# Attention steps of a fused kernel: block sums sent on at once, x transposed ahead of P in eight steps, routing tables a step later

## The chip, the cores and the metric

The program runs on one core of a Trainium2 chip. The metric is device time in microseconds, the median of several executions. The engines are called here as in the profile: PE is TensorE (PEld its weight loads), DVE is VectorE, ACT is ScalarE, POOL is GpSimd, SP is SyncE, which issues most transfers.

## The reference

Windowed attention with block summaries, and then a mixture of experts on its output. Cut to what matters:

```
# attention: q, k, v are (4, 8, 768, 64); block 32, window 16
k_sum = max over each block of 32 keys;  v_sum = mean over each block of 32 values
scores = [ scale*q@k.T where |i-j| < 16 else -1e9 ,  scale*q@k_sum.T + log(32) ]
a = softmax(scores);  x = a @ concat(v, v_sum)          # then (3072, 512)
# experts: w1 (8, 512, 1024), w2 (8, 1024, 512)
noisy = x@w_gate + log1p(exp(x@w_noise)) * noise
top2, weights = the two largest of 8 per row, softmax over the two
out[row] += weight * (relu(x[row] @ w1[e]) @ w2[e])     # for both experts of the row
```

## The kernel before, in words

**Steps.** The 3072 rows are 24 tiles of 128 (6 tiles for each of 4 batches). The attention part is a loop over steps `t`. In a step TensorE does, in this order: masks and scores of tile `t+2` (`mask_sums`, `scores`, L316 and L326), `av(t)` (P times V, 32 matmuls, L364), extras, the transposition of P of tile `t+1` (`p_trans`, two halves, L347), and the transposition of the finished x of tile `t-1` (`x_pe`, L418), each of which ScalarE copies out of PSUM (L350, and `x_copy`, L424). VectorE does the maxima for the softmax of tile `t+2` (`smax`, L335, L336), the division of tile `t` (`norm`, L395 to L399: r, ri, x) and extras. ScalarE does the exponentials (`sexp`, L341). GpSimd copies local keys and splits x into two halves (`norm_hi`, `norm_lo`, L405, L410). SyncE issues, in program order, the loads of q (`load_q`), of the value rows of tile `t+2` (`v_load`, L296, L297), and the write of finished x to memory (`x_out(t-2)`, L413). PSUM tiles for `p_trans`, `x_pe` and some extras come from a ring of three (`pt_space`).

**Extras** are hung on steps by a table, `at(step + fraction, function, ...)`. `run(step + fraction)` calls them at set places of the step; the fraction chooses the place, .4 and .1 are VectorE's (`.4` woven with `norm`, `.1` behind it). They are:
- For each of batches 1 to 3: key maxima (`k_piece`, `kmax`, L232, steps `KP`), loads of all value rows (`load_vn`, in the tile `hth`, L145, steps `VL`), the block sums of values by 48 small matmuls (`v_sums_pe`, L266, steps `VS`), their copy by ScalarE (`v_sums_out`, L278), and one transfer that repeats them for the other window slots (`v_rest`, `vw<-vw` or `htl<-htl`, L288). `av` of the batch's first tile (6, 12, 18) needs them.
- The weights of the first expert: `w_load(0, i)` loads, `w_part` splits into a high half on ScalarE (L736) and a low one on VectorE (L734).
- The routing of each four tiles: logits by TensorE (`gate_gt`, L438, in steps 5, 9, 13, 17, 21, and `gate_gl`, L449, a step later), the choice of two experts (`gate_b`, `gate_m`, L477 to L500), positions (`gate_c` to `gate_e`, L514 to L559, then `gate_q` on GpSimd), and a table product that sorts rows by expert: `lh` (L591), `oc` (L623), `rh` (L630) on VectorE, `gate_t` (L642) on TensorE, `gate_u` (L646, adds to `acc`) on VectorE.
- When three tables are in, `decode` (L653 to L659) gives the row numbers of the first expert's first three groups of 128; `x_gather` fetches those rows (an indirect transfer by GpSimd, `xg<-xd`, L94), `x_trans` transposes them by a transfer (`xte<-xg`, L861). The first expert's matmuls (L883) start behind the loop and read `xte`.

Behind that, eight experts follow one another, TensorE's matmuls back to back. None of it is touched.

Of the kernel before, what the change touches and what calls it, by code (L numbers as in the profile page):

```python
# [21 lines left out]
P = 128  # L22
# [29 lines left out]
GROUP0 = 3  # L52
# [10 lines left out]
def attn_moe(ctx, tc, qt, kt, vt, wgn, noise, w1, w2, out):  # L63
# [517 lines left out]
    GR = {}  # L581

    def gate_lh(b, h=0):
        if h and b == LASTB:
            lh = HT[0][:, :, H0:H0 + P]
        else:
            lh = work.tile([P, 2 * GN, P], F16, name="lh", bufs=1)
        GR[b, h] = [lh]
        shape = [P, 2 * GN, P // 2, 2]
        rf = G[b][2][:, GN * h:GN * h + GN].rearrange("p t k two -> p (t k) two")  # L590
        nc.vector.tensor_tensor(lh.rearrange("p a (c two) -> p a c two", two=2),  # L591
                                pairs_of(iotar)[:, None].to_broadcast(shape),
                                rf[:, :, None, :].to_broadcast(shape), op=OP.is_equal)
# [19 lines left out]
    def gate_o(b, h=0):  # L613
        val, qf, rf = G[b]
        oc = work.tile([P, GN, 2, NS], F16, name="oc", bufs=1)
        if h and b == LASTB:
            rh = HT[1][:, :, H0:H0 + 3 * NS]
        else:
            rh = work.tile([P, 2 * GN, 3 * NS], F16, name="rh", bufs=1)
        ic = iotac.rearrange("p e c -> p (e c)")  # L620
        qk = qf[:, GN * h:GN * h + GN].rearrange("p t k two -> p (t k) two")
        shape = [P, 2 * GN, NS // 2, 2]
        nc.vector.tensor_tensor(oc.rearrange("p t k (c two) -> p (t k) c two", two=2),  # L623
                                pairs_of(ic)[:, None].to_broadcast(shape),
                                qk[:, :, None, :].to_broadcast(shape), op=OP.is_equal)
        GR[b, h] += [rh, oc]

    def gate_f(b, h=0):
        _, rh, oc = GR[b, h]
        nc.vector.tensor_tensor(  # L630
            rh, oc.rearrange("p t k c -> p (t k) c")[:, :, None, :].to_broadcast([P, 2 * GN, 3, NS]),
            G[b][0][:, GN * h:GN * h + GN].rearrange("p t k v two -> p (t k v) two")[:, :, None, :].to_broadcast(
                [P, 6 * GN, NS // 2, 2]), op=OP.mult)

    def gate_t(b, o, hs=(0,), i=1):
        tb = o[:, i, GO:GO + 3 * NS]
        n = 2 * GN * len(hs)
        for h in hs:
            lh, rh, _ = GR[b, h]
            for j in range(2 * GN):  # L640
                n -= 1
                nc.tensor.matmul(tb, lh[:, j], rh[:, j], start=(h == hs[0] and j == 0), stop=(n == 0),  # L642
                                 skip_group_check=True)
# [448 lines left out]
    def at(t, f, *a):  # L1092
        todo.setdefault(round(t, 3), []).append((f, a))
# [23 lines left out]
    at(0.2, v_sums_out, 0)  # L1117

    w_alloc(0)
    for i, (l, h, z) in enumerate(((6, 8, 9), (7, 9, 10), (15, 19, 20), (16, 20, 21))):  # L1120
        at(l, w_load, 0, i)
        for k in range(2):
            at(h + 0.9, w_part, i, k, 0)
            at(z + 0.1, w_part, i, k, 1)
    VS = [4, 9, 15]
    KP = ((1, 1, 2, 2), (5, 6, 7, 8), (10, 12, 13, 14))
    KL = ((-1, 0), (3, 5), (9, 10))
    VL = [(1, 2), (6, 7), (12, 13)]
    for b in range(B - 1):
        for h in range(HP):  # L1130
            at(KP[b][h] + 0.1, k_piece, b + 1, h)
            if h % 2 == 0:
                at(KL[b][h // 2], load_k, b + 1, h, 2)
        for i in range(2):
            at(VL[b][i], load_vn, b + 1, i)
        at(VS[b] + 0.3, v_sums_pe, b + 1)
        at(VS[b] + 0.35, v_sums_out, b + 1)
        at(VS[b] + 1.02, v_rest, b + 1)
    for i in range(4, 8):
        at((17.9, 18.9, 21.9, 22.9)[i - 4], w_load, 0, i)  # L1140
    for i in range(3):
        at(4.9 + 2 * i, fill, i)
    at(20.8, last_init)
# [7 lines left out]
    def choose(b, t, m, c):  # L1151
        at(4 * b + 6 + 0.6, gate_a, b)
        if t == m:
            at(t + 0.4, lambda b: both(gate_b(b), gate_m(b)), b)
        else:
            at(t + 0.4, gate_b, b)
            at(m + 0.4, gate_m, b)
        at(m + 0.9, gate_p, b)
        at(c + 0.3, lambda b, t: gate_c(b, PO[t]), b, c)
        at(c + 0.4, lambda b, t: both(gate_d(b, PO[t]), gate_e(b)), b, c)  # L1160
        at(c + (1.7 if b < 1 else 0.7), gate_q, b)
# [2 lines left out]
        for g in gens:  # L1164
            yield from g

    choose(0, 7, 8, 9)
    choose(1, 11, 12, 13)
    choose(2, 15, 15, 16)
    choose(3, 20, 21, 22)  # L1170

    def make_table(b, v, lh, oc, rh):
        at(v + 0.8, gate_v, b, False)
        at(lh + 0.1, gate_lh, b)
        at(oc + 0.1, gate_o, b)
        at(rh + 0.1, gate_f, b)
        at(rh + 1.3, lambda b, t: gate_t(b, PO[t], (0,)), b, rh + 1)
        at(rh + 1.4, lambda b, t: gate_u(b, PO[t]), b, rh + 1)

    make_table(0, 10, 11, 11, 12)  # L1180
    make_table(1, 13, 14, 14, 15)
    make_table(2, 16, 17, 17, 18)
    at(19.1, decode, TB0, 0, 3)
    at(22.6, gate_a, 4)
    at(22.8, gate_v, 3, False)

    def run(t):
        for f, a in todo.pop(round(t, 3), []):
            f(*a)
# [13 lines left out]
        weave(small, more)  # L1203

    for c in range(3):
        at((20.25, 20.25, 20.7)[c], x_gather, 0, c, P * BATCH[GROUP0][0])
        at((21.02, 21.02, 21.8)[c], x_trans, 0, c)

    HI_ACT = ()

    for t in range(-2, NT - 1):
        u = t + 3
        if 4 <= t + QA < NT:
            load_q(t + QA)
        if 1 <= t < NT - 2:
            v_load(t + 2)
        if t >= 2:
            x_out(t - 2)
        run(t + 0.02)
        if t + 2 < NT:  # L1220
            mask_sums(t + 2)
            scores(t + 2)
        if 1 < u < NT and t < 1:
            q_piece(u)
        if u < NT and t >= 1:
            kx_sum(u)
            kx_local(u)
        run(t + 0.25)
        if t >= 1:
            norm_hi(t - 1, t - 1 not in HI_ACT)  # L1230
            norm_lo(t - 1)
        if t + 2 < NT:
            smax(t + 2)
        if t == 0:
            p_trans(1, 0)
            p_trans(1, 1)
        run(t + 0.2)
        if t >= 0:
            av_space(t)
            av(t)  # L1240
        run(t + 0.3)
        if t + 2 < NT:
            sexp(t + 2, 0)
        run(t + 0.35)
        if t == -1 or t > 0:
            p_trans(t + 1, 0)
            p_trans(t + 1, 1)
        if t >= 1:
            x_pe(t - 1)
        run(t + 0.09)  # L1250
        if t + 2 < NT:
            sexp(t + 2, 1)
        vector_work(t)
        if t >= 1:
            x_copy(t - 1)
        run(t + 0.6)
        run(t + 0.7)
        run(t)
        run(t + 0.8)
        run(t + 0.9)  # L1260
        run(t + 0.95)
# [311 lines left out]
```

## Time and profile before

| what | us |
|---|---|
| median of 3 runs (lowest, highest) | 650.5 (649.82, 651.01) |
| profiled execution, its own time | 652.03 |
| its span, first to last instruction | 650.2 |
| TensorE busy | 627.2 (96%) |
| VectorE busy | 480.0 (74%) |
| ScalarE busy | 306.3 (47%) |
| GpSimd busy | 351.3 (54%) |

The mean granted clock of TensorE was 0.997 of full speed. The loop with the 24 steps takes about the first 132 us. The busy shares are means over parts with different limits: what the loop waits for has to be read from the loop's own rows.

### The profile page before, as it was taken

How to read it: one execution, taken by the hardware profiler on the slowest of the kernel's cores; microseconds unless marked ns; L12 is line 12 of the kernel's file. 1: busy time of each engine (PE TensorE's matmuls, PEld its weight loads, DVE VectorE, ACT ScalarE, POOL GpSimd, SP SyncE). 2: the span in 40 equal slices, each digit the busy share in tenths (PEclk: the TensorE clock that was granted, in tenths of full speed). 3: DMA queues.
4: the chain of work that ended last, by engine and by line, in shares of the span. 5: the costliest groups of instructions: out<-in, count | busy, mean ns of one | idle time of the engine just before them, and what ended most of it. 6: DMA issues, size and time to landing. Idle time of an engine off the chain costs nothing.

```text
span 650.2 us, 14115 instructions
## 1 busy us (share of the span) xinstructions
PE 627.2 (96%) x5407; PEld 369.2 (57%) x5407; DVE 480.0 (74%) x897; ACT 306.3 (47%) x647; POOL 351.3 (54%) x531
## 2 busy tenths in 40 slices
PE   8888888989999999999999999999999999999996
PEld 7777777755555554554455446544554555455543
DVE  7756998987787789587957795788678677856511
ACT  4687777952532553265236523542464155315400
POOL 5575677743836558563765365555556451632042
PEclk9999999999999999999999999999999999999999
DMA  9999998899998676456835573667267723431021
GB/s 316 350 303 363 314 306 276 208 335 307 270 187 173 199 193 178 170 177 159 202 127 189 154 230 125 188 157 242 90 184 164 235 69 113 146 128 49 2 97 55
DMA packets 104568, 125.63 MB, mean 193 GB/s; under 512 B 58393, under 2 KB 59681, under 8 KB 104492
## 3 DMA queue, kind: packets, MB, share of 16 engines
q1 hardware_dynamic: 92348, 88.37, 46.6%
q0 software_dynamic: 12144, 36.28, 17.5%
q8 instruction: 44, 0.72, 0.5%
q14 instruction: 32, 0.26, 0.1%
HBM read 87.38 MB, written 26.21 MB: 175 GB/s over the span
## 4 chain that ended last, share of the span: by engine, by line
PE 74%; issue 8%; DVE 8%; DMA 4%; POOL 3%; ACT 1%; POOLq 1%; SPq 0%; DVEq 0%; ACTq 0%
PE pt L1038 33%; PE h L919 23%; PE h L883 4%; PE a L919 4%; PE pt L1035 3%; PE o L364 2%; DMA hth<-in_vt_dram 2%; PE s L326 1%; DVE s L335 1%; POOL prev L94 1%; PE pt L347 1%; ACT p L341 1%; DVE kmax L232 1%; PE h L1038 1%; DMA xg<-xd,tb 1%
## 5 line engine op out<-in xcount | busy, mean ns | idle before, releaser
L94 POOL DMA_INDIRECT out_dram<-y,tb x48 | 65.8, 1371 | 151.4 <-DVE y L1061 140.7
L1038 PEld LDWEIGHTS <-hth 128*128 128x128 f16 x768 | 74.9, 98 | 89.1
L94 POOL DMA_INDIRECT xg<-xd,tb x53 | 71.2, 1344 | 33.5 <-DMA out_dram<-prev 17.5
L1038 PE MATMUL pt<-w2l,hth 128*128 128x512 f16 x376 | 88.8, 379 | 0.0
L1038 PE MATMUL pt<-w2h,hth 128*128 128x512 f16 x376 | 88.8, 379 | 0.0
L1038 PE MATMUL pt<-w2h,htl 128*128 128x512 f16 x376 | 88.8, 379 | 0.0
L919 PE MATMUL h<-tx,sh 128*128 128x402 f16 x336 | 77.8, 333 | 0.0
L1061 DVE SCALAR_TENSOR_TENSOR y<-pt,tb,prev 128x512 f32<-128x512 f32 x42 | 31.5, 749 | 52.4 <-PE pt L1038 52.4
L741 DVE SCALAR_TENSOR_TENSOR w2l<-stg,w2h 128x1024 f16<-128x1024 f32 x32 | 48.7, 1531 | 28.4 <-ACT w2h L724 28.4
L341 ACT ACTIVATE p<-s,nm 128x120 f32<-128x120 f32 x188 | 53.2, 389 | 25.9 <-DVE nm L336 20.9
L1038 PEld LDWEIGHTS <-htl 128*128 128x128 f16 x384 | 37.5, 98 | 45.3
L919 PEld LDWEIGHTS <-w1h 128*128 128x128 f16 x448 | 43.1, 97 | 33.0 <-issue 1.4
L94 POOL DMA_INDIRECT prev<-out_dram,tb x42 | 51.9, 1236 | 13.6 <-issue 13.6
L788 POOL TENSOR_TENSOR t<-xte 128x804 f32<-128x804 f16 x24 | 38.9, 1645 | 36.7 <-DVE t L744 31.5
L919 PE MATMUL h<-xte,w1h 128*128 128x402 f16 x224 | 56.3, 333 | 0.0
L941 ACT ACTIVATE p<-h 128x402 f32<-128x402 f32 x28 | 14.2, 507 | 74.0 <-PE h L919 72.4
L816 ACT ACTIVATE tx<-t 128x804 f16<-128x804 f32 x28 | 23.7, 869 | 50.4 <-DVE t L744 50.4
L919 PEld LDWEIGHTS <-sh 128*128 128x128 f16 x336 | 32.6, 97 | 24.8
L919 PE MATMUL h<-tx,sl 128*128 128x402 f16 x168 | 42.2, 332 | 0.0
L335 DVE TENSOR_REDUCE s<-s 128x4 f32<-128x480 f32 x47 | 30.9, 658 | 10.1 <-PE s L326 9.8
L927 DVE SCALAR_TENSOR_TENSOR htl<-h,hth 128x402 f16<-128x402 f32 x56 | 31.9, 570 | 8.4 <-ACT hth L924 8.3
L769 ACT ACTIVATE sh<-ws 128x1536 f16<-128x1536 f32 x14 | 20.8, 1482 | 36.2 <-DVE ws L744 28.1
(240 smaller groups left out, 1238.4 us busy)
## 6 DMA issues: line engine op xcount, KB each, us to landing
stg<-in_w_dram SPq DMA_DIRECT2D x62, 512.0 KB, 4.2
q<-in_qt_dram SPq DMA_DIRECT2D x24, 256.0 KB, 6.3
hth<-in_vt_dram SPq DMA_DIRECT2D x8, 768.0 KB, 8.5
xd<-xr SPq DMA_DIRECT2D x24, 256.0 KB, 5.1
out_dram<-prev SPq DMA_DIRECT2D x8, 768.0 KB, 5.3
kb<-in_kt_dram SPq DMA_DIRECT2D x6, 768.0 KB, 6.1
htl<-in_vt_dram SPq DMA_DIRECT2D x12, 260.0 KB, 6.8
vw<-in_vt_dram SPq DMA_DIRECT2D x12, 260.0 KB, 7.8
```

The source lines that it names most:

```text
L94: return nc.gpsimd.indirect_dma_start(**kw)
L335: nc.vector.tensor_reduce(m, SC[t, a], axis=AX.X, op=OP.max)
L341: nc.scalar.activation(PE_[t, a][:, hp, :], SC[t, a][:, hp, :], AF.Exp, bias=NM[t][:, a, hp:hp + 1], scale=SCALE)
L741: nc.vector.scalar_tensor_tensor(lo, SG[e, i], sc, hi, op0=OP.mult, op1=OP.subtract)
L769: nc.scalar.activation(h, x, AF.Copy, scale=W1S)
L788: nc.gpsimd.tensor_tensor(tt(e, 0 if low else j), xb(e, *i, low), xb(e, *o, low), op=OP.subtract)
L816: nc.scalar.activation(TX[e][:, 0, j - 1], t_of(e, j), AF.Copy)
L883: nc.tensor.matmul(ph[:, :n], w[wn][:, c, f * P:(f + 1) * P], x[:, xo + c, c0:c1], start=(k == 0), stop=(k == 11), skip_group_check=hook i ...
L919: nc.tensor.matmul(o, lhs[a][:, c], rhs[b][:, c], start=start and n == 0, stop=stop and n == 5, skip_group_check=True)
L927: nc.vector.scalar_tensor_tensor(HT[1][:, f, c0:c1], c, 0.0, HT[0][:, f, c0:c1], op0=OP.max, op1=OP.subtract)
L1038: nc.tensor.matmul(py, hx[:, f, c * P:c * P + P], w[:, f, :], start=first, stop=final, skip_group_check=True)
L1061: nc.vector.scalar_tensor_tensor(y, py[:, :d], gw, pv[:, :d], op0=OP.mult, op1=OP.add)
```

## The change

Nothing is added or taken out; work is placed elsewhere.
- `v_rest` goes from the step behind the sums (fraction 1.02) to their own step (0.36), directly behind ScalarE's copy. The sums of the third batch (`VS[1]`) go from step 9 to step 10; its load stays.
- In eight steps (4, 5, 9, 10, 13, 15, 17, 21) `x_pe` and `x_copy` stand ahead of `p_trans`.
- VectorE's extras: the first table's parts go from steps 11, 11, 12 to 13, 14, 15, the second's from 14, 14, 15 to 16, 17, 17, the third's from 17, 17, 18 to 18, 18, 19; choices and positions from 7, 8, 9 to 9, 9, 10 (batch 0), 11, 12, 13 to 11, 13, 15, and 15, 15, 16 to 15, 16, 17. One key maximum goes from step 6 to 5. Splits and loads of the first expert's weights are later and further apart.
- `decode` goes from step 19 to 20, the gathers from 20 (the third late in it) to 21, their transposes from 21 to 22, where a new `run(t + 0.01)` puts them ahead of `x_out`.

```
     w_alloc(0)
-    for i, (l, h, z) in enumerate(((6, 8, 9), (7, 9, 10), (15, 19, 20), (16, 20, 21))):
+    for i, l in enumerate((7.8, 10.8, 14, 16)):
         at(l, w_load, 0, i)
-        for k in range(2):
-            at(h + 0.9, w_part, i, k, 0)
-            at(z + 0.1, w_part, i, k, 1)
-    VS = [4, 9, 15]
-    KP = ((1, 1, 2, 2), (5, 6, 7, 8), (10, 12, 13, 14))
+    for i, k, h, z in ((0, 0, 9, 10), (0, 1, 9, 10), (1, 0, 13, 18), (1, 1, 13, 19), (2, 0, 17, 21), (2, 1, 17, 21),
+                       (3, 0, 20, 22), (3, 1, 20, 22)):
+        at(h + 0.9, w_part, i, k, 0)
+        at(z + 0.1, w_part, i, k, 1)
+    VS = [4, 10, 15]
+    KP = ((1, 1, 2, 2), (5, 5, 7, 8), (10, 12, 13, 14))
...
         at(VS[b] + 0.35, v_sums_out, b + 1)
-        at(VS[b] + 1.02, v_rest, b + 1)
+        at(VS[b] + 0.36, v_rest, b + 1)
     for i in range(4, 8):
-        at((17.9, 18.9, 21.9, 22.9)[i - 4], w_load, 0, i)
+        at((17.9, 19.9, 22.8, 22.9)[i - 4], w_load, 0, i)
...
-    choose(0, 7, 8, 9)
-    choose(1, 11, 12, 13)
-    choose(2, 15, 15, 16)
+    choose(0, 9, 9, 10)
+    choose(1, 11, 13, 15)
+    choose(2, 15, 16, 17)
     choose(3, 20, 21, 22)
...
-    make_table(0, 10, 11, 11, 12)
-    make_table(1, 13, 14, 14, 15)
-    make_table(2, 16, 17, 17, 18)
-    at(19.1, decode, TB0, 0, 3)
+    make_table(0, 11, 13, 14, 15)
+    make_table(1, 15, 16, 17, 17)
+    make_table(2, 17, 18, 18, 19)
+    at(20.1, decode, TB0, 0, 3)
...
-        at((20.25, 20.25, 20.7)[c], x_gather, 0, c, P * BATCH[GROUP0][0])
-        at((21.02, 21.02, 21.8)[c], x_trans, 0, c)
+        at(21.25, x_gather, 0, c, P * BATCH[GROUP0][0])
+        at(22.01, x_trans, 0, c)
...
+    EXTRA = sorted(set(VS + [4 * g + 5 for g in range(5)]))
...
+        run(t + 0.01)
         if t >= 2:
             x_out(t - 2)
...
+        run(t + 0.36)
+        if t in EXTRA:
+            x_pe(t - 1)
+            x_copy(t - 1)
         if t == -1 or t > 0:
             p_trans(t + 1, 0)
             p_trans(t + 1, 1)
-        if t >= 1:
+        if t >= 1 and t not in EXTRA:
             x_pe(t - 1)
...
-        if t >= 1:
+        if t >= 1 and t not in EXTRA:
             x_copy(t - 1)
```

The rest of the diff lets `GR` hold a table's parts by name, so that `lh` and `oc` can be made in any order.

What this does to the instructions of an engine shows in the engine's own order. On SyncE, at the block sums of the second batch (steps 4 and 5; L288 is `v_rest`, L118 a load of q, L296 and L297 a `v_load`, L413 an `x_out`):

```order
 L413 DMA xd<-xr 128x1024
+L288 DMA vw<-vw 24x5x520
 L118 DMA q_101<-in_qt_dram 128x512
 L296 DMA vw<-in_vt_dram 64x2x520
 L297 DMA vw<-in_vt_dram 32x2x520
 L413 DMA xd<-xr 128x1024
-L288 DMA vw<-vw 24x5x520
```

`v_rest` moved ahead of one query block's load, one `v_load` and one `x_out`.

On VectorE, around `decode` (L646 is `gate_u`, L395 to L399 the division, L477 to L485 the choice of batch 3, L653 to L659 the decode). Before, in step 19:

```order
L646 TENSOR_TENSOR acc<-acc,o 128x168
L395 TENSOR_SCALAR r<-o 128x8
L397 RECIPROCAL ri<-r 128x8
L399 TENSOR_TENSOR x<-o,ri 128x512
L653 SCALAR_TENSOR_TENSOR oc<-acc 128x3
```

After, in step 20:

```order
L646 TENSOR_TENSOR acc<-acc,o 128x168
L395 TENSOR_SCALAR r<-o 128x8
L477 TENSOR_TENSOR nz<-sp,noi 128x32
L397 RECIPROCAL ri<-r 128x8
L479 SCALAR_TENSOR_TENSOR nl<-lg,nz 128x32
L399 TENSOR_TENSOR x<-o,ri 128x512
L482 MAX mx<-nl 128x8 x4
L485 MAX_INDEX ix<-mx,nl 128x8 x4
L653 SCALAR_TENSOR_TENSOR oc<-acc 128x3
```

The decode stands a step later, and the choice of batch 3, which was in step 20 already, now stands ahead of it.

On GpSimd, the three gathers of the first expert (L94), among the splits of x (L405, L410) and three small fills (L829 to L831). Before:

```order
L94 DMA xg_157<-xd,tb_173 128x1024
L93 MEMSET spacer 1x1
L94 DMA xg_158<-xd,tb_173 128x1024
L405 CAST xr<-x 128x512
L410 TENSOR_TENSOR xr<-x,xr 128x512
L93 MEMSET spacer 1x1
L94 DMA xg_159<-xd,tb_173 128x1024
```

After:

```order
L94 DMA xg_157<-xd,tb_173 128x1024
L93 MEMSET spacer 1x1
L94 DMA xg_158<-xd,tb_173 128x1024
L93 MEMSET spacer 1x1
L94 DMA xg_159<-xd,tb_173 128x1024
```

The third gather no longer stands behind a split of x; all three stand a step later.

## Rows read from the trace of the kernel before

**Rows 1.** Busy time by stretch: stretch, length, PE, PEld, DVE, ACT, POOL, clock, DMA share, GB/s.
```profile
150.00:165.00 15.00, 15.00 (x88) 7.83 (x86) 9.54 (x22) 2.61 (x5) 8.06 (x11) 1.00 0.90 286
```
**Rows 2.** TensorE's timeline in the loop: start, length, instructions, idle before and releaser.
```profile
46.22 1.15 PE L364 MATMUL o<-vw,pts 120*64 120x65 f32 x30 [1.61 <-DMA vw<-vw]
...
61.77 0.96 PE L266 MATMUL pt<-hth 128*24 128x130 f32 x25 [1.70 <-DMA hth<-in_vt_dram]
...
71.07 0.66 PE L418 MATMUL pt<-ident,x 128*128 128x128 f32 x4 [0.90 <-ACT lg L454]
...
81.00 0.35 PE L316 MATMUL s<-mask,identb 64*64 64x384 bf16 x2 [1.09 <-ACT p L341]
...
82.38 1.15 PE L364 MATMUL o<-htl,pts 120*64 120x65 f32 x32 [0.20 <-issue]
...
114.23 1.15 PE L364 MATMUL o<-vw,pts 120*64 120x65 f32 x32
...
118.42 1.15 PE L364 MATMUL o<-vw,pts 120*64 120x65 f32 x32
...
132.60 0.81 PE L883 MATMUL s<-xte,w1h 128*128 128x384 f16 x4 [0.17 <-DMA xte<-xg]
```
**Rows 3.** The chain that ended last: start, length, what.
```profile
41.01 5.17 DMA vw<-vw
...
51.81 9.92 DMA hth<-in_vt_dram
...
123.24 5.29 DMA xg<-xd,tb
128.54 4.02 DMA xte<-xg
```
**Rows 4.** VectorE's timeline in the loop.
```profile
71.46 1.28 DVE L734 SCALAR_TENSOR_TENSOR w1l<-stg,w1h 128x512 f16<-128x512 f32 x2
...
83.16 1.75 DVE L630 TENSOR_TENSOR rh<-oc,val 128x1344 f16<-128x1344 f16 x1
...
99.49 0.85 DVE L630 TENSOR_TENSOR rh<-oc,val 128x1344 f16<-128x1344 f16 x1
...
116.35 0.16 DVE L395 TENSOR_SCALAR r<-o 128x8 f32<-128x8 f32 x1
...
117.46 0.15 DVE L653 SCALAR_TENSOR_TENSOR oc<-acc 128x3 f32<-128x3 f32 x1
...
120.17 0.15 DVE L395 TENSOR_SCALAR r<-o 128x8 f32<-128x8 f32 x1
...
122.10 2.11 DVE L734 SCALAR_TENSOR_TENSOR w1l<-stg,w1h 128x512 f16<-128x512 f32 x2
```
**Rows 5.** SyncE's timeline, the issue of the repeated sums.
```profile
41.01 0.97 SPq L288 DMA_DIRECT2D vw<-vw  x1
```
**Rows 6.** ScalarE's timeline, its copy of the second batch's sums.
```profile
36.76 1.11 ACT L278 ACTIVATE vw<-pt 24x130 f32<-24x130 f32 x4 [0.38 <-PE pt L266]
```
**Rows 7.** Busy time by stretch (columns as in rows 1), in the loop.
```profile
44.30:46.20 1.90, 0.31 (x6) 0.17 (x2) 1.56 (x4) 1.46 (x6) 1.90 (x4) 1.00 0.88 278
59.95:61.75 1.80, 0.12 (x5) 0.00 (x0) 0.00 (x0) 1.22 (x6) 1.72 (x4) 1.00 1.06 353
62.80:66.00 3.20, 3.20 (x42) 2.77 (x35) 1.14 (x6) 1.49 (x6) 0.00 (x0) 0.50 1.01 294
82.38:118.42 36.04, 32.73 (x709) 27.98 (x709) 32.14 (x98) 28.52 (x94) 25.70 (x50) 1.00 0.85 281
```
**Rows 8.** The same table from the start on, for the last two columns.
```profile
0.00:62.00 62.00, 53.58 (x1113) 45.17 (x1117) 44.31 (x132) 42.30 (x132) 40.25 (x88) 1.00 1.00 334
0.00:75.00 75.00, 65.68 (x1340) 55.77 (x1341) 54.20 (x156) 51.88 (x162) 45.46 (x101) 0.98 1.00 332
75.00:80.00 5.00, 4.86 (x86) 3.86 (x85) 4.93 (x24) 3.29 (x11) 4.84 (x9) 1.00 1.01 293
```
**Rows 9.** GpSimd's timeline, the second gather.
```profile
120.18 1.00 POOL L94 DMA_INDIRECT xg<-xd,tb  x1 [0.20 <-issue]
```

More of the change, by code (lines that the diff above doesn't have):

```diff
@@ L587, in gate_lh @@
             lh = work.tile([P, 2 * GN, P], F16, name="lh", bufs=1)
-        GR[b, h] = [lh]
+        GR.setdefault((b, h), {})[0] = lh
         shape = [P, 2 * GN, P // 2, 2]
@@ L625, in gate_o @@
                                 qk[:, :, None, :].to_broadcast(shape), op=OP.is_equal)
-        GR[b, h] += [rh, oc]
+        GR.setdefault((b, h), {}).update({1: rh, 2: oc})
     def gate_f(b, h=0):
-        _, rh, oc = GR[b, h]
+        rh, oc = GR[b, h][1], GR[b, h][2]
         nc.vector.tensor_tensor(
@@ L638, in gate_t @@
         for h in hs:
-            lh, rh, _ = GR[b, h]
+            lh, rh = GR[b, h][0], GR[b, h][1]
             for j in range(2 * GN):
```

## The prediction

> **What bounds the kernel now.** Three views in this order. First the page's busy table: TensorE is busy for nearly the whole span, so a microsecond is won only where TensorE stands still. Then the busy table by stretch: from 150 us on TensorE is full (15.00 of 15.00 us) [rows 1], and the chain that ended last stays on its matmuls from there. What the change touches is ahead of that, the 24 attention steps, which end when the first expert matmul starts at 132.60 us [rows 2]. If that start moves, the end moves with it; nothing later is edited. Third, the chain and the engines' timelines inside the loop. The chain leaves TensorE at three kinds of place: two transfers, `vw<-vw` from 41.01 and `hth<-in_vt_dram` from 51.81 [rows 3]; VectorE, for most of 66 to 101 us (`rh`, 1.75 us at 83.16, is one of its pieces) [rows 4]; and, last, the gather of the first expert's rows and its transposition, 5.29 and 4.02 us, which release the first expert matmul [rows 3]. So that matmul, the exit of the loop, hangs on routing work, not only on the loop: it waited 0.17 us for `xte` [rows 2].
>
> I number steps by `av(t)`, the 32 matmuls of L364: step 13 starts them at 82.38, step 19 at 114.23, step 20 at 118.42 [rows 2].
>
> **Block sums.** `v_rest(1)` (L288) was issued at 41.01 [rows 5], behind `x_out(3)` on SyncE, which waits for GpSimd. The sums that it copies were written by ScalarE at 36.76 plus 1.11, so by 37.9 [rows 6]. In the new order it stands ahead of the next step's loads and can go at about 38. With its own 5.17 us [rows 3] it lands at about 43.2, before `av(6)` asks, at about 44.6. Gain: the 1.61 us of idle at 46.22 [rows 2]. The price is that on SyncE the loads of one query block and of `v_load(7)` now stand behind a wait until 38; they are asked for 10 us later, so I put it at nothing.
>
> **The third batch's sums, a step later.** In step 9 the sums wait for their load: TensorE idles 1.70 us to 61.77 [rows 2], and then its granted clock is 0.50 for 62.80 to 66.00 [rows 7], which is 1.2 instead of 2.4 GHz: 3.2 us of work at half rate, 1.6 us lost. In step 10 the same load is due a step later (one step is some 4.2 us, 114.23 to 118.42 [rows 2]) and has fewer bytes ahead of it, since both weight loads now stand behind it. Gain: 3.3 us; 1.7 at least, if only the idle goes. Their matmuls move and cost the same. Together with the last part 4.9 us, and TensorE's waits for ScalarE behind a late VectorE add 2.0 (0.90 before 71.07, 1.09 before 81.00 [rows 2]); with work moved out of steps 9 to 12 both may go. By TensorE and VectorE alone, `av(13)` could start 6.9 earlier, at about 75.5.
>
> **What the transfers allow.** The queue is full: share 1.00 from 0 to 75 us and 1.01 from 75 to 80 [rows 8]. Transfers queued up to and with the third batch's load, by their shapes, are 19.7 MB; it landed at 61.77, when 62 x 0.334 = 20.7 MB had moved [rows 8]: 1.0 MB goes on things that I don't count. Up to `v_load(13)` both orders queue the same set, 24.9 MB. So it lands when 25.9 MB have moved: 24.9 by 75 us, and 1.0 more at 0.293 MB per us, 3.5 us: 78.5 [rows 8]. The stretch before 46.2, where the share was 0.88 [rows 7], may give 0.5 back: 78.0. Step 13 can't start its `av` before. Between 75.5 and 78.0 the later one decides: **step 13 gains 4.4 us** (82.38 to 78.0), bounds 3.8 and 6.9. TensorE then waits in steps 10 to 13 for value rows, where it waited for VectorE.
>
> **Extras by room, tables later, steps 13 to 20.** Before, these seven steps took 36.04 us with TensorE busy 32.73 and VectorE 32.14 [rows 7]. The new order leaves in them: one table product less (to step 20), `decode` and one block maximum less, but one more pair `lh`/`oc` and two weight halves. For VectorE that is about 32.1 - 0.3 - 1.2 - 0.9 + 1.6 + 0.4 + 1.3 = 33.0 (one add into `acc`, the decode, one `kmax`, `lh` with `oc`, one choice, two halves). Before, no sequence of the two engines was without loss: the larger engine's work fell short of the span by 3.3. A more even spread should save part of it: I take 34.2, a gain of 1.8; bounds 33.0 (gain 3.0) and 36.0 (none). Step 20 then starts at 78.0 + 34.2 = 112.2: **6.2 us earlier** than 118.42.
>
> **x ahead of P in eight steps.** In such a step four or five PSUM tiles are taken from a ring of three, and the fourth waits for ScalarE to read the first. Before, the fourth was x; now it is P's second half, so TensorE's wait is the same; ScalarE copies P one copy of x later, and P's product comes only behind the next step's masks and scores. I cost it at nothing; if that cover is gone, a place costs at most what the ring's longest wait cost, the 0.90 before 71.07 [rows 2]. The later w1 loads lie under the same cover of steps: nothing.
>
> **The exit.** Here the change moves work on the path. `gate_t(2)`, the decode, the three gathers and the transposes all come one step later, in steps 20 to 22, while the expert's first matmul stays where it was. Before, from `av(19)` to that matmul: 132.60 - 114.23 = 18.37 us [rows 2]. What alters in this chain: the third gather no longer stands behind the two halves of x, so it starts at about 121.5 and not 123.24, 1.7 less [rows 9, 3]. But in step 20 the decode stands behind the choice of batch 3: from r to what follows took 1.93 us with it (120.17 to 122.10) and 1.11 without (116.35 to 117.46) [rows 4], 0.8 more. New chain: 18.37 - 1.74 + 0.82 = 17.45 us from `av(20)`. Before, from `av(20)` to the matmul it was 14.18 [rows 2]. So **the exit gives 3.3 us back**, and TensorE stands idle before the first expert matmul for some 3.4 us or more (bounds on the loss: 2.2 if the gathers land sooner, 4.5 if VectorE runs late in step 19). On SyncE the transposes now stand ahead of `x_out(20)` and two weight loads, on GpSimd the gathers ahead of both halves of that x; only gathers and splits behind the loop ask for these, so nothing for it.
>
> **The clock behind that wait.** Rows first. 1.8 us with TensorE busy 0.12 was followed by 3.2 us at 0.50; a stretch as long and busy 0.31, before 46.2, was not [rows 7]. A wait of 3.4 us and more is longer than both, so I take the fall. There it cost 1.6 us, all behind the wait; here part of the low stretch may lie inside the longer wait, so I take **1.2 us**; bounds 0 and 1.6. The Trainium skill, TensorE: Matmul & The Clock Gate (Part 1, the HAM clock gate), says that the gate sets the rate by how busy the array has lately been, and that the lower one follows idleness. By that rule the exit is at half rate and the sum is 648.8; by the row at 46.2 alone it stays and the sum is 647.6.
>
> **Sum.** 4.4 + 1.8 - 3.3 - 1.2 = 1.7 us. The profiled execution took 652.03 (span 650.2 and 1.8 around it), 1.5 above the median of the runs; I take the difference off the median: 650.5 - 1.7 = **648.8 us**.
>
> **Rivals.**
> *The exit costs less.* The clock stays, or gathers land sooner, or the transfers hold step 13 less. For it: a 1.8 us stretch left the clock at 1.00. Against: the exit's idle is longer. Clock alone: 647.6. With the loss at 2.2 as well: 646.5. With step 13 at 75.5 instead of 78.0: 644.0.
> *No change.* The even spread saves nothing, because step after step now stands at the transfers' pace or at VectorE's: 0 in place of 1.8. Then 4.4 - 3.3 - 1.2 = -0.1: 650.6. For it: VectorE's work in steps 13 to 20 rises to 33.0. Against: the transfers' share was 0.85 there [rows 7].
> *Slower: VectorE late in step 19.* The table's last operand, `rh`, now stands behind a weight half in the step before its product, where it had a step of room. Everything at the exit hangs on it. The same `rh` took 0.85 us at one place and 1.75 at another, a pair of weight halves 1.28 and 2.11 [rows 4]; three tables and a pair at the long price are 3 x 0.9 + 0.8 = 3.5 us late: 652.3. From 3.0 us of lateness on it is slower by over 0.2%. The Trainium skill, SBUF — State Buffer (two separate sides), says that VectorE with two SBUF inputs and GpSimd lock each other out of one port pair; by that rule the long `rh` is one that met GpSimd's work, and step 19 has x's two halves on GpSimd.
> That the change doesn't do what it says I leave out: the orders show every move.
>
> **Chances.** 0.2% (1.3 us) is about what a measurement of this kernel can tell from no change; it means below 649.2 or above 651.8. Forecast 0.40, own range 647.5 to 650.0, some seven tenths of it below 649.2; exit cheaper 0.30; no change 0.18, some of it beyond either bound; slower 0.12. So faster 0.28 + 0.30 = 0.58; same 0.12 + 0.16 = 0.28; slower 0.14. The range runs from 644.5 (near the cheapest sum) to 651.5 (a lateness of 2.7 us).
>
> **What would show it.** Right: no idle before `av(6)` and before the third batch's sums; no clock of 0.50 at 62 us; waits for value rows at step 12 or 13; `av(13)` near 78 and `av(20)` near 112; then a wait of 3 to 5 us of the first expert matmul for `xte`, which starts near 129.6 to 130, and a clock of 0.50 behind it. Wrong: `av(13)` at 75 or before (transfers don't hold), `av(20)` after 115 (no room gained), or no wait at the exit, which would mean that the table chain is shorter than its parts here.

## The result and the profile after

The changed kernel is slower: 657.04 us (655.24 to 659.91, nine runs) against 650.5 (648.76 to 652.52, nine runs on the same chip), ratio 1.0106, 95% interval 1.0088 to 1.0125. The profiled execution took 659.48 us, its span is 657.6 (before 650.2): 7.4 longer. Runs of this kernel spread over 4.7 us, so the profiled one is a long one among them, by some 2.4 us over the median.

Of each kernel there is one profile, so a stage that differs by less than a microsecond or two between two kernels may differ by chance; the times come from all runs.

TensorE's timeline of the changed kernel, with the places that answer to [rows 2]:

```profile
45.49 1.32 PE L364 MATMUL o<-vw,pts 120*64 120x65 f32 x32
...
64.99 1.07 PE L266 MATMUL pt<-hth 128*24 128x130 f32 x27
66.42 0.85 PE L266 MATMUL pt<-hth 128*24 128x130 f32 x21 [0.37 <-issue]
...
74.91 0.35 PE L316 MATMUL s<-mask,identb 64*64 64x384 bf16 x2 [1.31 <-ACT p L341]
...
80.68 1.43 PE L364 MATMUL o<-htl,pts 120*64 120x65 f32 x32 [0.78 <-DMA htl<-in_vt_dram]
...
90.44 1.15 PE L364 MATMUL o<-htl,pts 120*64 120x65 f32 x32
91.53 1.51 PE L266 MATMUL pt<-hth 128*24 128x130 f32 x42
95.33 0.42 PE L266 MATMUL pt<-hth 128*24 128x130 f32 x6 [2.29 <-issue]
...
119.52 0.35 PE L316 MATMUL s<-mask,identb 64*64 64x384 bf16 x2 [1.35 <-ACT p L341]
...
120.61 1.15 PE L364 MATMUL o<-vw,pts 120*64 120x65 f32 x32
...
137.82 1.44 PE L883 MATMUL s<-xte,w1h 128*128 128x384 f16 x4 [3.06 <-DMA xte<-xg]
```

The two idles that the change was to remove are gone: `av(6)` (45.49) waits for nothing, and the third batch's sums (64.99) wait 0.37 us instead of 1.70. But step 13 starts at 80.68, only 1.70 earlier than before, and step 20 at 120.61, 2.19 later. (The first `av` itself is at 19.80 here and at 19.07 before; over all twenty profiles it lies between 18.95 and 20.06. Where kernels are compared below, times in the loop are counted from it.) In the fourth batch's sums, at 93.04, TensorE stands 2.29 us for something that the profile does not name. The first expert matmul waits 3.06 us for `xte`. The same kernel by stretch (columns as in [rows 1]):

```profile
65.00:70.00 5.00, 4.19 (x84) 3.26 (x85) 2.32 (x9) 3.06 (x11) 3.17 (x6) 1.00 0.90 309
70.00:75.00 5.00, 3.69 (x80) 3.15 (x73) 4.92 (x12) 3.03 (x12) 2.67 (x6) 1.00 0.88 244
95.00:100.00 5.00, 4.67 (x61) 3.88 (x63) 3.25 (x24) 3.61 (x11) 1.98 (x7) 0.66 0.33 78
...
80.68:120.61 39.93, 33.99 (x700) 29.09 (x700) 31.74 (x98) 29.38 (x93) 26.89 (x51) 0.96 0.76 256
134.76:137.82 3.06, 0.00 (x0) 0.10 (x1) 2.48 (x9) 1.12 (x2) 2.56 (x9) 0.82 1.08 259
137.82:141.82 4.00, 4.00 (x14) 2.34 (x14) 0.00 (x0) 0.39 (x1) 2.56 (x5) 0.50 0.90 251
```

Three things to see. The transfers' share is 0.90 and 0.88 over 65 to 75 us, where the prediction counted on a full queue (before, the two together had 1.05). Steps 13 to 20 take 39.93 us (36.04 before [rows 7]), part of it at a low clock (0.66 over 95 to 100): TensorE is busy 1.26 us longer there than before and idle 2.63 us longer. Behind the wait for `xte` the clock is 0.50, which is 1.2 GHz.

So the 7.4 us split up without a rest: step 13 1.70 earlier; steps 13 to 20 3.89 longer; from `av(20)` to the first expert matmul 17.21 instead of 14.18, 3.03 longer; and from that matmul to the end 519.8 instead of 517.6 (span minus its start), 2.2 longer. 1.70 - 3.89 - 3.03 - 2.2 = -7.42.

Why step 13 came so little earlier is written in the chain that ended last (start, length, what):

```profile
66.42 0.91 PE pt L266 x21
67.41 0.27 ACT htl L278
...
69.28 0.16 SPq L288
...
69.54 0.46 SPq L112
...
70.05 1.37 SPq L715
...
71.47 0.47 SPq L118
71.98 0.70 SPq L296
72.73 7.82 DMA htl<-in_vt_dram
...
80.68 0.65 PE o L364 x15
```

Read it backwards. `av(13)` waits for its value rows. Their load was issued at 71.98 to 72.73, as late as that because SyncE issues in program order and stood at `v_rest(2)` (L288), which had to wait until ScalarE had copied sums that TensorE finished at about 67.3. (By the profile its releaser is the copy of x, L424, but it was issued at 68.55, as soon as the copy of the sums ended: 67.41 and 1.11 us.) Behind it stood the key load (L112), a weight load (L715), q and the rows. SyncE's own timeline shows the hole, 65.7 to 68.55, a second one for the fourth batch's sums, and a third, ahead of 120.68, in which a weight load (L718) waits 6.1 us for a buffer that VectorE's late weight half (L734) frees:

```profile
65.34 0.37 SPq L413 DMA_DIRECT2D xd<-xr  x1
68.55 0.88 SPq L288 DMA_DIRECT2D htl<-htl  x1
...
92.11 0.38 SPq L413 DMA_DIRECT2D xd<-xr  x1
96.97 0.87 SPq L288 DMA_DIRECT2D vw<-vw  x1
...
113.78 0.68 SPq L413 DMA_DIRECT2D xd<-xr  x1
120.68 0.38 SPq L718 DMA_DIRECT2D stg<-in_w_dram  x1
```

VectorE in step 10 and in step 20, which belongs to the exit, and GpSimd's third gather:

```profile
67.68 0.17 DVE L395 TENSOR_SCALAR r<-o 128x8 f32<-128x8 f32 x1 [2.69 <-PE o L518]
...
69.04 2.68 DVE L734 SCALAR_TENSOR_TENSOR w1l<-stg,w1h 128x512 f16<-128x512 f32 x2
71.64 0.94 DVE L232 TENSOR_REDUCE kmax<-kb 128x24 f32<-128x768 f32 x1
72.50 0.65 DVE L335 TENSOR_REDUCE s<-s 128x4 f32<-128x480 f32 x1
...
123.30 0.32 DVE L646 TENSOR_TENSOR acc<-acc,o 128x168 f32<-128x168 f32 x1
123.53 0.16 DVE L395 TENSOR_SCALAR r<-o 128x8 f32<-128x8 f32 x1
...
125.47 0.14 DVE L653 SCALAR_TENSOR_TENSOR oc<-acc 128x3 f32<-128x3 f32 x1
...
129.48 1.45 POOL L94 DMA_INDIRECT xg<-xd,tb  x1 [0.22 <-issue]
```

In step 10 VectorE first waits 2.69 us, because the positions of batch 0 (L518) now stand on TensorE behind the 48 matmuls of the sums, and then has two weight halves and a key maximum (3.5 us together) ahead of the softmax maxima: hence the 1.31 at 74.91. At the exit the table is complete at 123.62 and the decode starts at 125.47, behind the choice of batch 3.

### The profile page after: what moved, and what is told of

Its sections match the earlier page's. It is cut to its first block, busy times and chain, and to the rows that moved or that the text cites. A ratio compares the mean times of both kernels' runs of the same rounds, so it can differ in the third digit from the quotient of the medians.

```text
span 657.6 us, 14115 instructions
## 1 busy us (share of the span) xinstructions
PE 631.5 (96%) x5407; PEld 372.2 (57%) x5407; DVE 481.7 (73%) x897; ACT 306.4 (47%) x647; POOL 352.6 (54%) x531
## 4 chain that ended last, share of the span: by engine, by line
PE 76%; issue 9%; DMA 4%; DVE 4%; POOL 4%; ACT 1%; SPq 1%; POOLq 1%; DVEq 0%; ACTq 0%
PE pt L1038 32%; PE h L919 23%; PE h L883 4%; PE a L919 4%; PE pt L1035 3%; PE o L364 2%; PE s L326 2%; PE pt L347 2%; DMA q<-in_qt_dram 1%; DMA htl<-in_vt_dram 1%; POOL prev L94 1%; PE o L248 1%; DMA vw<-in_vt_dram 1%; DMA xd<-xr 1%; PE h L1038 1%
## 5 line engine op out<-in xcount | busy, mean ns | idle before, releaser
L94 POOL DMA_INDIRECT out_dram<-y,tb x48 | 65.8, 1371 | 151.5 <-DVE y L1061 140.7
L94 POOL DMA_INDIRECT xg<-xd,tb x53 | 72.0, 1358 | 34.2 <-DVE oc L658 20.9
L94 POOL DMA_INDIRECT prev<-out_dram,tb x42 | 51.8, 1233 | 13.6 <-issue 13.6
```

Of the source, the lines that this page charges most:

```text
L94: return nc.gpsimd.indirect_dma_start(**kw)
```

## The experiments

Times are ratios to the kernel before, from runs on the same chip, with 95% intervals. Theory A: the loss is made at the exit and on SyncE. Theory B: VectorE's new extras cost it.

**One part alone, on the kernel before.** Four runs: `v_rest` early, third batch's sums a step later, x ahead of P, and all that moves VectorE's extras, weights, tables and exit.

```
only_rest:     at(VS[b] + 1.02, v_rest, b + 1)  ->  at(VS[b] + 0.36, v_rest, b + 1)
only_vs10:     VS = [4, 9, 15]  ->  [4, 10, 15]
only_x_first:  the EXTRA list with its two places in the loop
only_tables:   KP, w_load, w_part, choose, make_table, decode, x_gather, x_trans
```

> The kernel before with one part of the change: the block sums are sent on at once (fraction 0.36). Theory A (the loss is made at the exit, by tables a step later, and at SyncE, where the early transfer waits for ScalarE ahead of the loads): the 1.61 us before av(6) goes, but SyncE stands still behind the transfer at the third and fourth batch, so little is left: 649 to 651. Theory B (VectorE's extras are what costs, SyncE's order is harmless): the whole 1.6 us shows, 648.9.

> The kernel before with one part: the third batch's sums in step 10 instead of 9. Both theories: the 1.70 us of idle and the 1.6 us of half clock at 62 us go. Theory A: the fourth batch's value load, which sits behind the same bytes as before, is then what holds TensorE in step 15, and gives 1 to 2 us back: 648 to 650. Theory B: VectorE, which is full from step 10 to 16, keeps all of it: 650.5.

> The kernel before with one part: x transposed ahead of P, in steps 4, 5, 9, 13, 15, 17, 21 (step 10 is not among them, as the third batch's sums stay in step 9). Prediction and theory A: nothing, 650.5 within 0.7. Theory B: nothing either. If it costs (over 652), P's later copies are on the path and a part of the loss is made here.

> The kernel before with one part: VectorE's extras dealt anew (choices, tables, key maximum, weight splits and loads), decode, gathers and transposes a step later. Theory A: all of the exit's loss is here, 3.3 us of longer chain and some 2 us of half clock behind the wait, and little else: 655 to 657, with a wait of about 3 us for xte before the first expert matmul. Theory B: the same and VectorE's waits in steps 12 and 19 on top: 657 to 660.

Measured: only_rest 1.0019 (1.0001 to 1.0037); only_vs10 1.0024 (1.0010 to 1.0038); only_x_first 0.9992 (0.9979 to 1.0004); only_tables 1.0046 (1.0023 to 1.0070). Three of the four parts are slower by themselves, only_rest by a hair; x ahead of P is nothing, as forecast. In only_rest neither 649 to 651 nor 648.9 came. only_tables came cheaper than either theory had it (655 or more; 1.0046 is 653.5): the wait for `xte` (2.90 us) and the low clock behind it are there as theory A had them, but step 20 starts 2.8 us earlier after the first `av` than before. In only_vs10 both expectations missed, since the repeated sums, sent a step later than the sums, now come too late for step 12:

```profile
79.40 1.99 PE L364 MATMUL o<-htl,pts 120*64 120x65 f32 x30 [3.98 <-DMA htl<-htl]
```

That is the dilemma of the third batch's moved sums: sent at once they hold SyncE and every load behind them, sent a step later they hold TensorE for 3.98 us.

**The exit alone as before.** The changed kernel with the third batch's choice and table, decode, gathers and transposes at their old steps.

```
choose(2, 15, 16, 17) -> (2, 15, 15, 16);  make_table(2, 17, 18, 18, 19) -> (2, 16, 17, 17, 18)
decode 20.1 -> 19.1;  x_gather 21.25 -> 20.25, 20.25, 20.7;  x_trans 22.01 -> 21.02, 21.02, 21.8
```

> The changed kernel, but the third batch's choice and table, the decode, the gathers and the transposes of the first expert's rows stand where they stood before, a step earlier. Theory A (the loss is made at the exit and where a load holds TensorE in step 15): the wait of about 3 us for xte and the half clock behind it go, the rest stays: about 5.0 us less than the changed kernel, 651 to 653 us, and av(20) stays within 1 us of where it was (120.6). Theory B (VectorE's new deal makes the loop late): VectorE gets a table's work back in steps 16 to 18, av(20) starts 1.5 us or more later, and the time falls by less than 3 us: 654 or above.

Measured: 1.0126 (1.0101 to 1.0151). Theory B's number came (654 or above, `av(20)` 4.9 us later), but not for its reason, and the edit is no clean test of the exit. The exit was short (15.5 us from `av(20)`), but VectorE stood in step 17:

```profile
113.77 1.54 DVE L591 TENSOR_TENSOR lh<-iotar,rf 128x1024 f16<-128x1024 f16 x1 [3.41 <-PE o L642]
```

`lh` has one buffer, and the second table's product, still at its new place, had not read it. TensorE then waited 3.56 us. The table dates hang together: moving the second table later forces the third, and with it the exit, later too.

**All choices, tables and the exit as before.** Block sums, x ahead of P and weights as changed.

```
choose(0, 7, 8, 9);  choose(1, 11, 12, 13);  choose(2, 15, 15, 16)
make_table(0, 10, 11, 11, 12);  make_table(1, 13, 14, 14, 15);  and the lines of the exit above
```

> The changed kernel, but all choices and tables, the decode, the gathers and the transposes stand where they stood before; block sums, x ahead of P and the weights stay changed. In the run with the exit alone as before, VectorE stood 3.4 us for the second table's product, because one buffer lh holds both tables; here the second table is a step or two earlier as well. Theory A (the exit is worth 5 us): 652 to 653.5, with av(20) within 1 us of 120.6. Theory B (VectorE has no room for the early tables beside the moved weights and the third batch's later sums): the loop loses what the exit wins, 656 to 659.

Measured: 1.0008 (0.9990 to 1.0027). Nearly the whole loss is gone, and more than theory A had expected (`av(20)` is at 116.63): beside the other parts, the later place of choices, tables and exit costs about 1.0% (6.4 us). By itself it had cost 0.46%, so the parts do not add up. By profile, step 20 starts 97.2 us after the first `av` (100.8 in the changed kernel, 99.3 before), the exit takes 15.2 and no low clock follows it (517.6). So 2.1 us are won in the loop against the kernel before, and 1.0 of it is lost again at the exit, in a wait of 1.83 us for `xte`.

Set beside the changed kernel, this run says where the loss lies: steps 13 to 20 take 35.85 us for 39.93, the exit 15.21 for 17.21, and from the first expert matmul to the end it is 517.6 for 519.8. Step 13 starts at 80.78, no earlier than the changed kernel's 80.68, and SyncE is held in the same way:

```profile
68.07 0.88 SPq L288 DMA_DIRECT2D htl<-htl  x1
...
65.00:75.00 10.00, 8.64 (x180) 7.33 (x181) 7.26 (x28) 7.59 (x26) 7.35 (x18) 1.00 0.89 274
```

So the hold of SyncE explains a gain that did not come, and not the loss: with it, but with choices, tables and exit at their old steps, the kernel is level with the one before.

**The fourth batch's load a step earlier,** by itself and with the exit alone as before.

```
VL = [(1, 2), (6, 7), (12, 13)]  ->  [(1, 2), (6, 7), (11, 12)]
```

> The changed kernel, but both loads of the fourth batch's hth are issued a step earlier (steps 11 and 12 for 12 and 13). Theory A (that load, behind a full queue, holds the block sums in step 15 for 2.3 us, and the half clock behind that costs 1.6): the stall in the middle of the L266 matmuls goes, the clock over 94 to 104 us is 1.00, and the time falls by 3 to 4 us: 653 to 654. If the queue gives TensorE only so many bytes by 95 us whatever the order, value rows wait instead, by about as long without the half clock: 655 to 656.5. Theory B (VectorE sets the steps): step 16 starts no earlier, 656 to 658.

> The two edits together: the exit as before, and the fourth batch's hth load a step earlier. Theory A: the two losses lie in different places and add up, 5 + 3.5 us less than the changed kernel: 648 to 649.5, under the kernel before. Theory B: 653 or above.

Measured: load_early 1.0093 (1.0058 to 1.0127), exit_and_load 1.0132 (1.0107 to 1.0157), the latter caught by the same `lh`. In load_early the unnamed wait within the sums shrinks from 2.29 to 0.71 and the clock does not fall:

```profile
94.87 0.42 PE L266 MATMUL pt<-hth 128*24 128x130 f32 x6 [0.71 <-issue]
```

So that wait was the load. Steps 13 to 20 take 37.21 us instead of 39.93. `av(16)` came 78.3 us after the first `av` instead of 80.1; other waits (1.21 at 82.4, 0.91 at 88.6) took some back. In the medians the gain of 0.13% is within the intervals.

**The fourth batch's repeated sums a step later,** as before.

```
at(VS[b] + 0.36, v_rest, b + 1)  ->  at(VS[b] + (0.36, 0.36, 1.02)[b], v_rest, b + 1)
```

> The changed kernel, but the fourth batch's repeated block sums (v_rest, L288) are sent on a step later, as before; those of the second and third batch stay early. Theory A (SyncE, which waits for them from 92.5 to 97.0 with loads behind it, is part of the loss): the loads of three query blocks and value rows go out 4.5 us earlier, the queue's share of 0.33 over 95 to 100 rises to 0.8 or more, and the time falls by 0.5 to 2 us. Rival: those loads are asked for later than they land either way: share rises and the time stays, 656 to 658.

Measured: 1.0098 (1.0075 to 1.0122), not to be told from the changed kernel. The share over 95 to 100 us rose from 0.33 to 0.86, the wait in the sums stayed (2.31): the rival's reading. No cost of the second hole on SyncE shows; its loads are asked for later.

**VectorE's weight halves elsewhere, and the last choice behind the decode.**

```
halves_moved:  (0,0,9,10), (0,1,9,10), (1,0,13,18), (1,1,13,19) -> (0,0,9,11), (0,1,9,12), (1,0,13,14), (1,1,13,16)
choice3_late:  choose(3, 20, 21, 22) -> choose(3, 21, 21, 22)
mended:        both, and the fourth batch's load a step earlier
```

> The changed kernel, but VectorE's weight halves w1l leave the steps where it has a choice or a table: the two of step 10 go to steps 11 and 12, those of steps 18 and 19 to steps 14 and 16. Theory C (VectorE's extras stand in the wrong steps: 2.68 us of halves ahead of the block maxima of step 10, 0.94 and 0.68 in steps 18 and 19): the two waits of the mask products for ScalarE's p (1.31 at 74.9, 1.35 at 119.5) go, SyncE no longer stands 6 us for a buffer in steps 19 and 20, av(20) starts 2 to 3 us earlier, and the time falls by as much: 655 to 656 where the changed kernel shows 657 to 659 on this chip. Rival (transfers hold the steps to 95 us, so that a wait saved at 75 comes back at the fourth batch's load): only the second wait is won, 1 us or less.

> The changed kernel, but the first part of the fourth batch's choice (noise, MAX8, indices) goes from step 20 to step 21, behind the decode. The decode ran 1.85 us after the accumulator was complete (123.62 to 125.47), behind that choice. Theory A (the exit hangs on the chain table, decode, gathers, transposition): decode, gathers and the first expert matmul come 1.5 to 1.8 us earlier, av(20) to that matmul takes 15.5 to 15.8 instead of 17.2, its wait for xte falls from 3.06 to about 1.3; the time falls by 1.5, and by up to 3.5 if the half clock behind it goes too: 654 to 656.5. Rival (gathers or their queue are the limit, not the decode): the wait stays at 2.5 or above and so does the time.

> The changed kernel with three edits together: the weight halves of the first run here, the choice behind the decode of the second, and the fourth batch's hth load a step earlier. If the losses are those three places and lie one after another: 2 to 3, 1.5 to 3.5 and 1 to 3 us less, so 649 to 652, about level with the kernel before. If a wait that is taken away returns at the next engine: 655 or above.

Measured: halves_moved 1.0071 (1.0047 to 1.0096), choice3_late 1.0080 (1.0052 to 1.0107), mended 1.0068 (1.0049 to 1.0087). With the halves moved, both mask waits are gone, steps 13 to 20 take 35.0 us, `av(20)` comes 2.5 us earlier and the median ratio falls by 0.35% (2.3 us; the intervals overlap): theory C's numbers. But step 13 is 2.4 us later after the first `av`, since TensorE now stands 2.14 us for q at 81.38 and 0.47 for rows; that a saved wait comes back at a transfer is the rival's part of it. The time of choice3_late lies in theory A's range, but its interval overlaps the changed kernel's, and A's path is not the one taken. With the choice later, the first gather starts 5.1 us behind `av(20)` instead of 6.0, but the first expert matmul still 17.5 behind it: the gain ends in the gathers, whose first takes 5.74 us. The choice's own product meanwhile waits for VectorE:

```profile
131.57 0.18 PE L514 MATMUL o<-m,tri 128*128 128x32 f16 x1 [1.46 <-DVE m L500]
136.76 0.81 PE L883 MATMUL s<-xte,w1h 128*128 128x384 f16 x4 [1.87 <-DMA xte<-xg]
```

The three gains do not add up: in mended no wait for `xte` is left, but 2.02 us for that product at 128.5 and a clock of 0.75 over 130 to 136.

**The wait taken off SyncE.** `v_rest` on ScalarE's queue, in the changed kernel and with tables as before; and the third gather ahead of a split of x.

```
rest_act:             nc.sync.dma_start(x[:, 1:6], ...) -> nc.scalar.dma_start(x[:, 1:6], ...)
tables_old_gather:    x_gather 20.25, 20.25, 20.7 -> 20.25 for all three
tables_old_rest_act:  tables_old and the first line;  tables_old_both: and the second too
```

> The changed kernel, but the repeated block sums (v_rest, L288) are sent by ScalarE's queue, right behind the evictions that write them, and not by SyncE's. Theory D (the wait on SyncE with loads behind it is why the loop's gain did not come): the queue's share over 65 to 75 us rises from 0.89 to 1.0 or more, the fourth batch's sums in step 15 wait 1 us or less instead of 2.3, av(16) starts 1.5 us or more earlier and the time falls by 1.5 to 4. Rival C (VectorE's lateness in steps 10 to 12 and 18 to 20 decides): the share rises, but av(20) stays within 1 us and the time too.

> Choices, tables and exit as before, the rest as changed, and v_rest on ScalarE's queue. Theory D: the wait of 1.54 us for q at 79.1 goes, av(13) starts near 79 instead of 80.8, av(20) near 115 instead of 116.6; but the first expert matmul waits for xte already, so the time falls only as far as the table chain moves with the steps: 0.997 to 0.999 of before. Rival: ScalarE, which now issues a transfer of its own, is late by as much: 1.000 to 1.002.

> Choices, tables and exit as before, the rest as changed, but the third gather is issued with the other two, ahead of GpSimd's two halves of x (0.62 and 1.17 us) that stood between them. Theory A (the loop's gain of 2 us is lost at the exit, in a wait of 1.83 us for xte behind the third gather): xte comes 1.8 us earlier, that wait falls to 0.3 or less, and the time falls by 1.5: 0.998 to 0.999 of before. Rival (the gathers share a full queue and land no sooner): the wait stays, 1.000 to 1.001.

> The last two edits together. If both theories hold, the loop's gain reaches the end: av(20) near 115, no wait for xte, 2 to 4 us less than the kernel before (0.994 to 0.997), which is what the forecast looked for. If ScalarE or the queue takes it back: 0.999 to 1.001.

Measured: rest_act 1.0129 (1.0109 to 1.0149), tables_old_rest_act 1.0077 (1.0054 to 1.0100), tables_old_gather 1.0034 (1.0018 to 1.0049), tables_old_both 1.0076 (1.0060 to 1.0091). All four expectations of a gain failed, though their first sign came: the share over 65 to 75 us rose from 0.89 to 0.97, 0.98 and 1.00 in the three runs with ScalarE's queue. SyncE's waits in rest_act (engine, line, releaser, us, times, longest) show why the first was no clean test:

```profile
SPq L118 <- DMA htl<-htl: 9.3, 1, 9.3
SPq L296 <- DMA vw<-vw: 6.1, 1, 6.1
SPq L413 <- DMA vw<-vw: 5.0, 1, 5.0
```

Put on ScalarE's queue, the transfer had to land before SyncE went on: three waits of 20.4 us together where L288 itself had waited 10.3. The share fell to 0.59 and 0.72 over 75 to 85 us. With the tables as before the same edit costs 0.7% (1.0008 to 1.0077): the wait for q at 79.1 is gone, as expected, but `av(12)` now waits 2.10 us for the repeated sums. A longer hold of SyncE costs more time: that fits the chain above, but no run shows what none would give. The Trainium skill, DMA: Bandwidth & Descriptors (Issuing engines are not separate DMA queues), says that transfers run on the same 16 engines whichever engine issues them, so no bandwidth was to be had. The trace agrees: in rest_act no stretch of 5 us from 60 to 120 us has a share over 1.05.

The third gather was issued 1.3 us after the second instead of 3.05, but it was the second that now ended last, after 6.93 us instead of the third's 5.43 (chain of tables_old_gather):

```profile
120.60 6.93 DMA xg<-xd,tb
...
128.87 3.95 DMA xte<-xg
```

**The third batch's load earlier instead of its sums later.** The kernel before with x ahead of P and `VL[1]` (5, 6) for (6, 7); early_load_w has the changed weights too.

> The kernel before with x ahead of P in eight steps, the changed places of the weights, and the third batch's hth load a step earlier (steps 5 and 6 for 6 and 7); sums, repeated sums, choices, tables and exit as before. Theory A (the stall in step 9 was a real loss of 3.3 us): no wait before the third batch's sums, clock 1.00 over 62 to 66, av(10) near 64.5 instead of 67.9 and av(20) 2 to 3 us earlier, the first expert matmul 1 to 2 earlier: 0.996 to 0.998 of before. Theory E (up to step 13 the queue is full, and the order within it only moves the wait): av(10) earlier, but waits for value rows or q in steps 10 to 13, av(13) at 81.5 or later and 0.999 to 1.001.

> The same without the changed places of the weights: both w1 loads are issued in steps 6 and 7, behind the third batch's load. Theory A: 0.996 to 0.999 of before. Theory E: as many bytes are ahead of step 13 as before and the weights' 1 MB comes ahead of the rows of steps 9 and 10, so waits for value rows from step 9 on, 1.000 to 1.002.

Measured: early_load_w 0.9995 (0.9971 to 1.0020), early_load 1.0003 (0.9981 to 1.0025). In early_load_w the stall in step 9 goes without a hold of SyncE, and step 20 starts 95.7 us after the first `av` (99.3 before), the earliest of all profiles, in spite of waits of 1.42 and 1.37 us in steps 10 and 12: the loop is as theory A had it or better, the time as theory E. The first expert matmul starts 2.5 us earlier than before, behind a wait for `xte`:

```profile
130.13 0.81 PE L883 MATMUL s<-xte,w1h 128*128 128x384 f16 x4 [1.67 <-DMA xte<-xg]
```

Of the 2.5 us, 1.1 go behind that matmul (518.7 to the end instead of 517.6). The medians do not show the rest. The two runs differ in the places of the weights alone, and their times can't be told apart. No version here is shown to beat the kernel before.

## Why the prediction was wrong

Forecast were gains of 4.4 and 1.8 us ahead of step 20 and costs of 3.3 and 1.2 behind it. The costs came, as 3.0 and 2.2. The gains did not: 1.7, and a loss of 3.9.

**The step that failed** is "Extras by room, tables later, steps 13 to 20": the stretch was taken as 34.2 with a worst of 36.0, because a more even spread "should save part" of what the two engines lose, and it took 39.93. That is 5.7 of the 9.1 us between the forecast (1.7 gained) and the profile (7.4 lost), and `av(20)` after 115 was the prediction's own sign of it. What the runs show in its place: with the same sums, the same hold of SyncE and the same weights, but choices, tables and exit at their old steps, the stretch takes 35.85. So, beside the moved sums, the later tables lengthened what they were to shorten; without the moved sums (only_tables) they left it at 36.09.

Of the 3.9 us over before, 2.8 fall ahead of `av(16)`. There TensorE waits 2.29 us for the fourth batch's load (shown by load_early), and its clock falls behind that; it gets to step 15 3.3 us earlier after the first `av` than before (70.6 for 73.9). That the stall removed in step 9 is paid there is not shown: in tables_old step 15 is early too (72.2) and meets no wait. The other 1.1 lie behind `av(16)`, with VectorE's lateness of 1.35 at 119.52 (shown by halves_moved, where it is gone) and 1.48 us within the scores at 110.37 that the profile does not name (0.93 at that place before). The rival "slower: VectorE late in step 19" named the first of these, but gave it 3.5 us and the whole loss. With the tables later, 35.0 us or less came only in halves_moved, where step 13 started no earlier after the first `av` than before; the three other profiles that short (34.2 to 34.9) had it no earlier either.

**The second miss** is the price of `v_rest` on SyncE, "nothing", and with it "what the transfers allow". I worked that price out for the second batch, where the sums are early, and did not look at the third, where the change itself had moved them to the end of step 10 and the queue was full. There SyncE stands 2.8 us with the key load and step 13's rows behind it, the queue runs at 0.89 instead of 1.05 for ten microseconds (1.6 us of it lost, by estimate), and step 13 starts at 80.68, not 78.0; 0.7 of that lies ahead of the first `av`. (In the sum itself, 1.0 MB at 0.293 takes 3.4 us and not 3.5.) That the hold is on the path is shown by the chain; what a loop without it would give is not, since neither the later place (3.98 us) nor the other queue (9.3 us) was free of a new wait.

**The exit** was right: 17.45 forecast, 17.21 measured; in the eight profiles with tables a step later it was 16.3 to 17.5, in the twelve others 13.8 to 15.7. Its two parts came as forecast: from r to the decode 1.94 us for 1.11 before, from the decode to the third gather 4.01 for 5.78. That the total fits as closely is luck, for two things that it did not have nearly cancel: r came 2.92 us behind `av(20)`, where it had been 2.12 behind `av(19)`, and from the third gather to the matmul it took 8.34 instead of 9.36. That it can't be bought back by the decode alone is shown by choice3_late.

**The clock** fell as forecast; the term was mis-sized: 2.2 instead of 1.2, more than the bound of 1.6 too. The mean of 0.82 over the wait shows that part of the low stretch did lie inside it, as assumed, but it went on for long enough behind it. **x ahead of P** cost nothing: right. **That the end moves with the first expert matmul**: right to 0.3 us wherever the clock stayed (517.4 to 517.9 in twelve profiles; 518.4 to 519.0 in five, each with one more wait of 0.6 to 1.4 us between 169 and 181 us, at the second pass over `xte`).

Two things stay open. Why is the fourth batch's load no hindrance with the tables as before, though it is issued at the same time (82.60 for 82.37 us)? TensorE comes to these sums 1.1 us later there (92.67 for 91.53), which is half of the 2.29; why the other half is gone is not shown. And what an unheld SyncE is worth is not shown either.

## What to carry to other kernels

Ahead of an in-order issuing engine, ask of a transfer that is moved earlier not only whether it is wanted sooner, but when its source is ready: each load behind it waits with it, and what the queue does not move meanwhile may be missing later (here some 1.6 us; the second such hold cost nothing that shows). A stall for a load that is taken away from one batch may be followed by one at the next batch whose load stands in the same queue, as here in step 15; look there too. Do not add up parts that were costed one by one: the change without the later choices, tables and exit measured 1.0008, these alone (with the key maximum and the weights) 1.0046, and the whole 1.0106. Before tables or other chains with one buffer are moved later, follow the last of them to the exit of the loop: what was spread evenly inside comes out late there.

## What the runs showed of the hardware

The clock's answer to an idle of the same place and kind differs from profile to profile. In the stretch ahead of the first expert matmul TensorE was idle 3.06 us (changed kernel) and 2.90 (only_tables) and ran on at 0.50, and idle 2.99 (rest4_old) and ran on at 0.62 over the next 4 us; in halves_moved it was idle for longer and stayed at 1.00, behind the same matmuls:

```profile
131.60:134.93 3.33, 0.00 (x0) 0.10 (x1) 2.75 (x10) 1.11 (x2) 2.75 (x10) 1.00 1.02 240
134.93:138.93 4.00, 4.00 (x52) 2.74 (x51) 0.89 (x2) 1.61 (x3) 2.90 (x6) 1.00 0.79 229
```

So did rest_act (3.33) and load_early (2.71). The price of the fall is 2.2 and 2.4 us in the first two (519.8 and 520.0 from the matmul to the end, 517.6 before); rest4_old's 520.6 has a later wait of 1.35 us in it too. The Trainium skill, TensorE: Matmul & The Clock Gate (Part 1), says that the gate's count runs freely, so that the same kernel meets it at different points; the rows fit that, and a forecast can give such a fall only a chance, not a certainty.
